# Adjacent heads on the two partition halves in a fused sigmoid attention and ReGLU kernel

## Chip, cores, metric

One core of one Trainium2 chip. The metric is the device time of one execution in microseconds (us).

## The reference, cut to what matters

```python
# q, k, v: [8 batches, 12 heads, 448, 64] fp32
scores = matmul(q, k.T) / sqrt(64) - log(448)
attn_out = matmul(1 / (1 + exp(-scores)), v)                  # no softmax, no row sums
x = attn_out.transpose(0, 2, 1, 3).reshape(3584, 768)         # heads side by side
out = (maximum(x @ w_gate, 0) * (x @ w_val)) @ w_out          # 768 -> 1536 -> 768
```

The head index is the upper part of the feature index of `x`. So heads 2j and 2j+1 together make up features 128j to 128j+127, one 128-row slice for the first matmul of the FFN.

## The kernel before

All matmuls are in fp16. For each batch the kernel loads k, q and v with a cast to fp16, transposes k and q, forms K·Qᵀ in 64x64 tiles (QK), applies the sigmoid on ScalarE (ACT), multiplies by v (PV), and mixes the FFN of an earlier batch into the gaps. Batch 0 has nothing to be mixed with: it runs as six "slots" of four QK units each, and FFN units (`"f"`: one 128-wide slice of the gate and value products) are placed among them by hand.

A tile holds two heads per partition half. Before, partitions 0 to 63 carry heads 0 to 5 and partitions 64 to 127 carry heads 6 to 11, so one load of a group of four heads is two transfers of 64 partitions:

```python
    def tiles_of(b):
        if b not in in_tiles:
            in_tiles[b] = tuple(
                inp.tile([P, NG, 2, NCH * D], FP16, tag=t, name=t) for t in ("k16", "q16", "v16")
            )
        return in_tiles[b]

    def rows_of(src, b, r, g0, g1, c0, c1):
        hs = src[b, 6 * r + 2 * g0 : 6 * r + 2 * g1]
        return hs.rearrange("h (t c) d -> t h (c d)", c=NCH)[:, :, c0 * D : c1 * D]

    def load(b, g0, g1, which="kqv", c0=0):
        for nm, t16, src in zip("kqv", tiles_of(b), (k, q, v)):
            if nm in which:
                for r in range(2):
                    nc.gpsimd.dma_start(
                        t16[64 * r : 64 * r + 64, g0:g1, :, c0 * D :].rearrange(
                            "t g h x -> t (g h) x"
                        ),
                        rows_of(src, b, r, g0, g1, c0, NCH),
                    )

    KCUT = 4                                   # the first k and q come as fp32 (QCUT is 3, NCH 7, D 64)
    first32 = []
    for src, c0, c1 in ((k, 0, KCUT), (q, 0, QCUT)):
        ysb = ysbp.tile([P, DM], FP32, tag="ysb", name="ysb")
        t32 = ysb[:, 0 : 2 * (c1 - c0) * D].rearrange("p (h x) -> p h x", h=2)
        for r, eng in ((0, nc.sync), (1, nc.scalar)):
            eng.dma_start(t32[64 * r : 64 * r + 64], rows_of(src, 0, r, 0, 1, c0, c1))
        first32.append(t32)
    # ... (constants)
    load(0, 0, 1, "k", KCUT)
    load(0, 1, 2, "kq")
    load(0, 2, 3, "kq")
    load(0, 0, 1, "q", QCUT)
    load(0, 0, 3, "v")
    # ... then the weights of the FFN by slices, with k and q of batch 1 between them
```

`load` issues everything on GpSimd's queue (POOL), in this order. A QK unit and a PV group use the four 64x64 quadrants of TensorE at once (in the profile of before, four PV matmuls of 448 columns start within 10 ns and the next four 189 ns later):

```python
    def qk(qkT, r, hh, c, c0, c1, out_ap):
        rows = slice(64 * hh, 64 * hh + 64)
        cols = slice(64 * r, 64 * r + 64)
        nc.tensor.matmul(
            out_ap,
            qkT[rows, c, cols],
            qkT[rows, NCH + c0 : NCH + c1, cols],
            start=True,
            stop=True,
            tile_position=(64 * hh, 64 * r),
            skip_group_check=True,
        )

    def pv(b, g, q0, qn, pieces):
        v16 = in_tiles[b][2]
        ps = [bank("pv_ps") for _ in range(2)]
        for c in range(NCH):
            for hh in range(2):
                for r in range(2):
                    rows = slice(64 * r, 64 * r + 64)
                    nc.tensor.matmul(
                        ps[r][64 * hh : 64 * hh + 64, 0:qn],
                        v16[rows, g, hh, c * D : (c + 1) * D],
                        pieces[c][rows, hh, :],
                        start=(c == 0),
                        stop=(c == NCH - 1),
                        tile_position=(64 * r, 64 * hh),
                        skip_group_check=True,
                    )
        for r in range(2):
            put_xT(b, NG * r + g, q0, qn, ps[r][:, 0:qn])
```

The places of PV and of FFN units among the six slots of batch 0 (transposes and warm-up matmuls cut):

```python
    push_first(0, range(0, 4), False)          # four FFN units for the first 192 rows
    after = {
        # ...
        (2, 2): slots[0].pv,
        (2, 3): slots[1].pv,
        (3, 1): slots[2].pv,
        (3, 3): lambda: ffn_mix("f"),
        (4, 0): lambda: ffn_mix("f"),
        (4, 1): slots[3].pv,
        (4, 3): lambda: ffn_mix("f"),
        (5, 0): lambda: ffn_mix("f"),
        (5, 1): slots[4].pv,
    }
    for i, slot in enumerate(slots):
        for u in range(4):
            slot.unit(u)
            if (i, u) in after:
                after[(i, u)]()
    slots[5].pv()
    # ...
    ffn_mix("ff", [(1, lambda: both(1, 0))])   # then batch 1
```

## Time and profile before

| kernel before | value |
|---|---|
| three timed executions | 433.53, 434.48, 434.69 us; median 434.48 |
| the profiled execution: time / span in the profile | 437.15 / 435.4 us |
| TensorE busy | 423.8 us, 97% of the span |
| first QK / fourth PV matmul ("full PV") / first FFN unit | 7.75 / 18.75 / 24.12 us |
| second half of v of batch 0 landed at | 18.71 us |

The span is what the profile covers, some 1.8 us less than the time of the same execution. TensorE works nearly all the time, so only its early holes can give anything; the "milestones" in the fourth row, taken from the start of the span, date them. PV of batch 0 starts with a few matmuls on the half of v that came first; the fourth needs the rest, so its start shows when v had landed.

### The profile page before, as it was taken

The numbers are of one execution on the slowest core, as the hardware profiler recorded it, in microseconds if no ns is written. First come the engines' busy times: TensorE is split into PE (matmuls) and PEld (weight loads), VectorE is DVE, ScalarE is ACT, GpSimd is POOL, SyncE is SP. The second block draws the span as 40 slices with busy tenths as digits, with TensorE's granted clock in tenths as the row PEclk, the third lists the DMA queues.
The fourth block names the chain that finished last, engine by engine and source line by source line (L and its number), as shares of the span: only waits on it lengthen the run. The fifth ranks groups of instructions, "written<-read, shape, count | busy, mean of one in ns | idle before, by whom it ended". The sixth has DMA issues, their size and how long they took to land.

```text
span 435.4 us, 8668 instructions
## 1 busy us (share of the span) xinstructions
PE 423.8 (97%) x3670; PEld 237.2 (54%) x3670; DVE 129.5 (30%) x246; ACT 212.0 (49%) x453; POOL 59.8 (14%) x97
## 2 busy tenths in 40 slices
PE   7789999999999999999999999999999999999996
PEld 3567776455555455455555555455555545555563
DVE  2243244222332323322332223323332222222111
ACT  4585778454554555654554635645654545122110
POOL 8555510621030000300030000100000000000000
PEclk9899999999999999999999999999999999999999
DMA  8999945999999043963259225631243101100144
GB/s 134 183 198 198 196 63 98 170 202 220 209 148 182 0 80 81 154 115 79 43 96 182 65 44 80 106 74 38 43 80 80 38 0 38 36 2 0 40 106 108
DMA packets 70214, 43.64 MB, mean 100 GB/s; under 512 B 35488, under 2 KB 66592, under 8 KB 70176
## 3 DMA queue, kind: packets, MB, share of 16 engines
q0 software_dynamic: 32128, 23.37, 36.6%
q1 hardware_dynamic: 37680, 19.44, 22.0%
q8 instruction: 28, 0.46, 0.4%
q10 hardware_dynamic: 368, 0.30, 0.3%
q14 instruction: 10, 0.08, 0.0%
HBM read 47.19 MB, written 11.01 MB: 134 GB/s over the span
## 4 chain that ended last, share of the span: by engine, by line
PE 93%; DMA 3%; ACT 1%; POOL 1%; DVE 1%; issue 1%; ACTq 0%; POOLq 0%
PE g_ps L292 26%; PE v_ps L292 25%; PE ya L330 17%; PE qk_ps L214 9%; PE yb L330 8%; PE pv_ps L231 7%; DMA v<-in_v_dram 2%; DMA k<-in_k_dram 1%; ACT PT L175 1%; DVE xT L166 1%; PE trt L189 1%; POOL k L97 0%; POOL v L97 0%; POOL q L97 0%; ACT ysb L344 0%
## 5 line engine op out<-in xcount | busy, mean ns | idle before, releaser
L175 ACT ACTIVATE PT<-qk_ps 128x448 f16<-128x448 f32 (+3 forms) x318 | 150.8, 594 | 38.3 <-PE qk_ps L214 38.3
L292 PE MATMUL g_ps<-xT,wg 128*128 128x448 f16 (+2 forms) x648 | 127.5, 332 | 0.6 <-DVE xT L166 0.4
L292 PE MATMUL v_ps<-xT,wv 128*128 128x448 f16 (+2 forms) x648 | 126.8, 332 | 0.0
L310 DVE TENSOR_TENSOR hT<-gate_sb,v_ps 128x448 f16<-128x448 f32 (+2 forms) x108 | 60.9, 568 | 195.7 <-PE v_ps L292 116.4
L301 ACT ACTIVATE gate_sb<-g_ps 128x448 f32<-128x448 f32 (+2 forms) x104 | 55.3, 543 | 74.7 <-PE g_ps L292 73.8
L330 PEld LDWEIGHTS <-hT 128*128 128x128 f16 x672 | 65.8, 98 | 47.0
L292 PEld LDWEIGHTS <-wv 128*128 128x128 f16 x648 | 62.5, 98 | 46.8
L292 PEld LDWEIGHTS <-wg 128*128 128x128 f16 x648 | 59.3, 98 | 49.2 <-issue 10.7
L330 PE MATMUL ya<-wo,hT 128*128 128x512 f16 x336 | 77.1, 379 | 0.0
L344 ACT ACTIVATE ysb<-yb 128x256 f32<-128x256 f32 x28 | 10.7, 383 | 102.1 <-PE yb L330 102.1
L214 PE MATMUL qk_ps<-qkT 64*64 64x448 f16 (+2 forms) x756 | 52.2, 339 | 2.3 <-ACT PT L175 1.3
L330 PE MATMUL yb<-wo,hT 128*128 128x256 f16 x336 | 41.3, 273 | 0.0
L231 PE MATMUL pv_ps<-PT,v 64*64 64x448 f16 (+2 forms) x756 | 38.3, 337 | 2.5 <-DMA v<-in_v_dram 2.1
L166 DVE TENSOR_SCALAR xT<-pv_ps 128x448 f16<-128x448 f32 (+2 forms) x54 | 28.4, 567 | 31.5 <-PE pv_ps L231 31.5
L214 PEld LDWEIGHTS <-qkT 64*64 64x64 f16 x756 | 21.3, 107 | 29.8 <-issue 21.2
L97 POOL DMA_DIRECT2D v<-in_v_dram x18 | 12.1, 680 | 177.4 <-PE qk_ps L214 169.7
L338 DVE TENSOR_SCALAR ysb<-ya 128x512 f32<-128x512 f32 x28 | 19.3, 691 | 55.2 <-PE ya L330 55.2
L231 PEld LDWEIGHTS <-v 64*64 64x64 f16 x756 | 22.6, 111 | 13.9 <-DMA v<-in_v_dram 2.5
L97 POOL DMA_DIRECT2D q<-in_q_dram x28 | 17.5, 644 | 7.1 <-DMA v<-in_v_dram 4.7
L97 POOL DMA_DIRECT2D k<-in_k_dram x28 | 17.5, 635 | 6.8 <-DMA wv<-in_moe_w_val_dram 3.8
L194 DVE COPY qkT<-trt 128x896 f16<-128x896 f16 (+2 forms) x14 | 7.5, 554 | 7.7 <-PE trt L189 7.5
L158 PE MATMUL warm_ps<-zeros 128*128 128x448 f16 x22 | 7.1, 451 | 1.2 <-DVE zeros L114 1.2
(24 smaller groups left out, 46.5 us busy)
## 6 DMA issues: line engine op xcount, KB each, us to landing
out_dram<-ysb SPq DMA_DIRECT2D x54, 192.0 KB, 2.7
v<-in_v_dram POOLq DMA_DIRECT2D x14, 336.0 KB, 7.0
k<-in_k_dram POOLq DMA_DIRECT2D x10, 336.0 KB, 9.0
q<-in_q_dram POOLq DMA_DIRECT2D x10, 336.0 KB, 13.4
wg<-in_moe_w_gate_dram POOLq DMA_DIRECT2D x6, 384.0 KB, 10.0
wv<-in_moe_w_val_dram POOLq DMA_DIRECT2D x6, 384.0 KB, 10.4
k<-in_k_dram POOLq DMA_DIRECT2D x16, 112.0 KB, 7.7
q<-in_q_dram POOLq DMA_DIRECT2D x16, 112.0 KB, 6.4
```

Of the source, the lines that this page charges most:

```text
L97: nc.gpsimd.dma_start(t16[64 * r : 64 * r + 64, g0:g1, :, c0 * D :].rearrange("t g h x -> t (g h) x"), rows_of(src, b, r, g0, g1, c0, NCH),)
L166: nc.vector.tensor_scalar(out=xT_of(b, pr)[:, q0 : q0 + qn], in0=src, scalar1=XSCALE, scalar2=None, op0=AOP.mult,)
L175: nc.scalar.activation(PT_ap, ps_ap, AF.Sigmoid, bias=sig_bias, scale=qk_scale)
L194: nc.vector.tensor_copy(qkT[:, ti * NCH + c0 : ti * NCH + c1, :].rearrange("p c x -> p (c x)"), trt[:, c0 * P : c1 * P],)
L214: nc.tensor.matmul(out_ap, qkT[rows, c, cols], qkT[rows, NCH + c0 : NCH + c1, cols], start=True, stop=True, tile_position=(64 * hh, 64 * r ...
L231: nc.tensor.matmul(ps[r][64 * hh : 64 * hh + 64, 0:qn], v16[rows, g, hh, c * D : (c + 1) * D], pieces[c][rows, hh, :], start=(c == 0), sto ...
L292: nc.tensor.matmul(ps[-1][:, 0:qn], wt[:, dc, f * P : (f + 1) * P], xT_tiles[(b, dc)][:, q0 : q0 + qn], start=(dc == 0), stop=(dc == NDC - 1),
L301: nc.scalar.activation(gate_sb[:, 0:qn], ps[0][:, 0:qn], AF.Relu)
L310: nc.vector.tensor_tensor(out=hT_tiles[(g, f)][:, o : o + qn], in0=gate_sb[:, 0:qn], in1=ps[1][:, 0:qn], op=AOP.mult,)
L330: nc.tensor.matmul(ps[:, 0 : m1 - m0], hT_tiles[(g, f)][:, t * P : (t + 1) * P], wo[:, f, m0:m1], start=(f == 0), stop=(f == NFC - 1),)
L338: nc.vector.tensor_scalar(out=ysb[:, m0:m1], in0=ps[:], scalar1=OUT_SCALE, scalar2=None, op0=AOP.mult)
L344: nc.scalar.activation(ysb[:, m0:m1], ps[:, 0 : m1 - m0], AF.Copy, scale=OUT_SCALE)
```

## The change

The intent is to let each k and q load cover all 128 partitions. Head 2x goes to partitions 0 to 63 and head 2x+1 to 64 to 127, so a group of heads is one transfer instead of two. The PV result of a pair of heads must land in the two halves of one PSUM tile. With v and the sigmoid on the same halves, that would use only the two diagonal quadrants. So odd pairs are exchanged: QK writes their results to the other partition half, and their v is loaded exchanged. In PV, both row halves now write the same PSUM bank, on different partitions. The patch also moves FFN work: six FFN units instead of four run among the first slots, two of them after the last QK unit, and one more before batch 1.

```diff
-                inp.tile([P, NG, 2, NCH * D], FP16, tag=t, name=t) for t in ("k16", "q16", "v16")
+                inp.tile([P, NPAIR, NCH * D], FP16, tag=t, name=t) for t in ("k16", "q16", "v16")
...
+    def rows_of(src, b):
+        return src[b].rearrange("(x r) (t c) d -> (r t) x (c d)", r=2, c=NCH)
...
-                for r in range(2):
-                    nc.gpsimd.dma_start(t16[64 * r : 64 * r + 64, g0:g1, ...], ...)
+                xs = slice(2 * g0, 2 * g1)
+                nc.gpsimd.dma_start(t16[:, xs, c0 * D :], rows_of(src, b)[:, xs, c0 * D :])
+
+    def load_v(b):
+        v16 = tiles_of(b)[2]
+        nc.gpsimd.dma_start(v16[:, 0::2, :], rows_of(v, b)[:, 0::2, :])
+        for r in range(2):
+            nc.gpsimd.dma_start(
+                v16[64 - 64 * r : P - 64 * r, 1::2, :], rows_of(v, b)[64 * r : 64 * r + 64, 1::2, :]
+            )
...  first fp32 loads: k whole on SP's queue, q whole on ACT's (were one half of each on both)
+    for src, c1, eng in ((k, KCUT, nc.sync), (q, QCUT, nc.scalar)):
...
+    load_gv(4, 6)
     load(1, 0, 1, "kq")
-    load_gv(4, 6)
...
+    def row_of(r, hh):
+        return 64 * (r if hh == 0 else 1 - r)
...  QK: output on partitions o = row_of(r, hh), tile position (64 * hh, o)
...  PV:
-                        ps[r][64 * hh : 64 * hh + 64, 0:qn],
-                        v16[rows, g, hh, c * D : (c + 1) * D],
+                        ps[hh][64 * r : 64 * r + 64, 0:qn],
+                        v16[rows, 2 * g + hh, c * D : (c + 1) * D],
-                        tile_position=(64 * r, 64 * hh),
+                        tile_position=(o, 64 * r),
...
-    push_first(0, range(0, 4), False)
+    push_first(0, range(0, 6), False)
...
-        (4, 3): lambda: ffn_mix("f"),
+        (4, 2): lambda: ffn_mix("f"),
         (5, 0): lambda: ffn_mix("f"),
         (5, 1): slots[4].pv,
+        (5, 3): lambda: ffn_mix("ff"),
...
-    ffn_mix("ff", [(1, lambda: both(1, 0))])
+    ffn_mix("fff", [(1, lambda: both(1, 0))])
...  batch 1: FFN units per stretch 3, 4, 3, 3, 2 instead of 4, 4, 3, 4, 3
...  loads of v and of the output weights for batch 2: v first
```

More of the change, by code (lines that the diff above doesn't have):

```diff
@@ L84, in tiles_of, with load @@
             in_tiles[b] = tuple(
-                inp.tile([P, NG, 2, NCH * D], FP16, tag=t, name=t) for t in ("k16", "q16", "v16")
+                inp.tile([P, NPAIR, NCH * D], FP16, tag=t, name=t) for t in ("k16", "q16", "v16")
             )
         return in_tiles[b]
-    def rows_of(src, b, r, g0, g1, c0, c1):
-        hs = src[b, 6 * r + 2 * g0 : 6 * r + 2 * g1]
-        return hs.rearrange("h (t c) d -> t h (c d)", c=NCH)[:, :, c0 * D : c1 * D]
-    def load(b, g0, g1, which="kqv", c0=0):
-        for nm, t16, src in zip("kqv", tiles_of(b), (k, q, v)):
-            if nm in which:
-                for r in range(2):
-                    nc.gpsimd.dma_start(
-                        t16[64 * r : 64 * r + 64, g0:g1, :, c0 * D :].rearrange(
-                            "t g h x -> t (g h) x"
-                        ),
-                        rows_of(src, b, r, g0, g1, c0, NCH),
-                    )
+    def rows_of(src, b):
+        return src[b].rearrange("(x r) (t c) d -> (r t) x (c d)", r=2, c=NCH)
+    def load(b, g0, g1, which, c0=0):
+        for nm, t16, src in zip("kq", tiles_of(b), (k, q)):
+            if nm in which:
+                xs = slice(2 * g0, 2 * g1)
[7 more added lines that the diff above has]
+            )
     KCUT = 4
     first32 = []
-    for src, c0, c1 in ((k, 0, KCUT), (q, 0, QCUT)):
+    for src, c1, eng in ((k, KCUT, nc.sync), (q, QCUT, nc.scalar)):
         ysb = ysbp.tile([P, DM], FP32, tag="ysb", name="ysb")
-        t32 = ysb[:, 0 : 2 * (c1 - c0) * D].rearrange("p (h x) -> p h x", h=2)
-        for r, eng in ((0, nc.sync), (1, nc.scalar)):
-            eng.dma_start(t32[64 * r : 64 * r + 64], rows_of(src, 0, r, 0, 1, c0, c1))
+        t32 = ysb[:, 0 : 2 * c1 * D].rearrange("p (x y) -> p x y", x=2)
+        eng.dma_start(t32, rows_of(src, 0)[:, 0:2, 0 : c1 * D])
         first32.append(t32)
@@ L122 @@
     load(0, 0, 1, "q", QCUT)
-    load(0, 0, 3, "v")
+    load_v(0)
     wg = wpool.tile([P, NDC, DF], FP16, name="wg")
@@ L142 @@
     load_gv(10, 12)
-    load(1, 0, 3, "v")
+    load_v(1)
     def load_o():
@@ L190, in pe_transposes @@
                     trt[64 * h : 64 * h + 64, c * P : (c + 1) * P],
-                    t16[:, g, h, c * D : (c + 1) * D],
+                    t16[:, 2 * g + h, c * D : (c + 1) * D],
                     ident[:],
@@ L204, in dma_transposes @@
                 rel[:, ti * NCH : (ti + 1) * NCH, :].rearrange("p c (h d) -> p h c d", h=2),
-                t16[:, g].rearrange("p h (c d) -> p h c d", c=NCH),
+                t16[:, 2 * g : 2 * g + 2, :].rearrange("p h (c d) -> p h c d", c=NCH),
             )
@@ L209, in dma_transposes, with qk @@
         )
-    def qk(qkT, r, hh, c, c0, c1, out_ap):
-        rows = slice(64 * hh, 64 * hh + 64)
-        cols = slice(64 * r, 64 * r + 64)
-        nc.tensor.matmul(
-            out_ap,
-            qkT[rows, c, cols],
-            qkT[rows, NCH + c0 : NCH + c1, cols],
-            start=True,
-            stop=True,
-            tile_position=(64 * hh, 64 * r),
-            skip_group_check=True,
-        )
+    def row_of(r, hh):
+        return 64 * (r if hh == 0 else 1 - r)
+    def qk(qkT, c, c0, c1, out_of):
+        for r in range(2):
+            for hh in range(2):
+                rows = slice(64 * hh, 64 * hh + 64)
+                cols = slice(64 * r, 64 * r + 64)
+                o = row_of(r, hh)
+                nc.tensor.matmul(
+                    out_of(hh)[o : o + 64, :],
+                    qkT[rows, c, cols],
+                    qkT[rows, NCH + c0 : NCH + c1, cols],
+                    start=True,
+                    stop=True,
+                    tile_position=(64 * hh, o),
+                    skip_group_check=True,
+                )
     def pv(b, g, q0, qn, pieces):
@@ L229, in pv @@
                 for r in range(2):
-                    rows = slice(64 * r, 64 * r + 64)
+                    o = row_of(r, hh)
+                    rows = slice(o, o + 64)
                     nc.tensor.matmul(
-                        ps[r][64 * hh : 64 * hh + 64, 0:qn],
-                        v16[rows, g, hh, c * D : (c + 1) * D],
+                        ps[hh][64 * r : 64 * r + 64, 0:qn],
+                        v16[rows, 2 * g + hh, c * D : (c + 1) * D],
                         pieces[c][rows, hh, :],
@@ L236, in pv @@
                         stop=(c == NCH - 1),
-                        tile_position=(64 * r, 64 * hh),
+                        tile_position=(o, 64 * r),
                         skip_group_check=True,
                     )
-        for r in range(2):
-            put_xT(b, NG * r + g, q0, qn, ps[r][:, 0:qn])
+        for hh in range(2):
+            put_xT(b, 2 * g + hh, q0, qn, ps[hh][:, 0:qn])
     class FirstSlot:
@@ L254, in unit @@
             for j, c in enumerate(cs):
-                for r in range(2):
-                    for hh in range(2):
-                        qk(
-                            qkT_tiles[(0, self.g)], r, hh, c, self.c0, self.c1,
-                            ps[64 * r : 64 * r + 64, hh, j * qn : (j + 1) * qn],
-                        )
+                qk(
+                    qkT_tiles[(0, self.g)], c, self.c0, self.c1,
+                    lambda hh: ps[:, hh, j * qn : (j + 1) * qn],
+                )
             PT = PTp.tile([P, 2, 512], FP16, tag="PT", name="PT")
@@ L274, in qk_unit @@
         ps = [bank("qk_ps") for _ in range(2)]
-        for r in range(2):
-            for hh in range(2):
-                qk(qkT_tiles[(b, g)], r, hh, c, 0, NCH, ps[hh][64 * r : 64 * r + 64, 0:S])
+        qk(qkT_tiles[(b, g)], c, 0, NCH, lambda hh: ps[hh][:, 0:S])
         PT = PTp.tile([P, 2, 512], FP16, tag="PT", name="PT")
@@ L377 @@
     k16, q16, _ = in_tiles[0]
-    nc.vector.tensor_copy(k16[:, 0, :, 0 : KCUT * D], first32[0])
-    nc.scalar.copy(q16[:, 0, :, 0 : QCUT * D], first32[1])
+    nc.vector.tensor_copy(k16[:, 0:2, 0 : KCUT * D], first32[0])
+    nc.scalar.copy(q16[:, 0:2, 0 : QCUT * D], first32[1])
     pe_transposes(0, 0, 0, 0, KCUT)
@@ L413 @@
     slots[5].pv()
-    push_first(1, range(0, 4))
-    for f0 in range(4, 12, 2):
+    push_first(1, range(0, 6))
+    for f0 in range(6, 12, 2):
         for half in range(2):
@@ L441, in late_loads @@
         hold(2, 1)
-        load(2, 0, 1, "v")
+        load_v(2)
         load_o()
-        load(2, 1, 3, "v")
-    ffn_mix("ff", [(1, lambda: both(1, 0))])
+    ffn_mix("fff", [(1, lambda: both(1, 0))])
     for b in range(1, B):
@@ L451 @@
         if b == 1:
-            mix = ["f" * n for n in (4, 4, 3, 4, 3)]
+            mix = ["f" * n for n in (3, 4, 3, 3, 2)]
             hooks = {
@@ L484 @@
                     hold(2, 2)
-                load(b + 1, 0, 3)
+                load(b + 1, 0, 3, "kq")
+                load_v(b + 1)
             ffn_mix(mix[m], hooks.get(m, ()))
```

## The prediction

> **What bounds the kernel now.** I read the page first: busy shares, the 40 slices, the chain that ended last. Its first and third parts say that TensorE is the bound for nearly the whole span, and its slices that DMA is busiest in the first eighth.
>
> ```profile
> span 435.4 us, 8668 instructions
> PE 423.8 (97%) x3670; PEld 237.2 (54%) x3670; DVE 129.5 (30%) x246; ACT 212.0 (49%) x453; POOL 59.8 (14%) x97
> PE   7789999999999999999999999999999999999996
> PE 93%; DMA 3%; ACT 1%; POOL 1%; DVE 1%; issue 1%; ACTq 0%; POOLq 0%
> ```
>
> The reader is to see that only the first three digits of the PE row, some 33 us, are under 9. The change removes no matmul, so a gain must come from there, or from a wait hidden inside a "busy" PE. To see which wait, I took the waits of PE and the timeline of PE for 17 to 22 us:
>
> ```profile
> PE pv_ps L231 <- DMA v<-in_v_dram: 2.1, 2, 1.1
> ...
> PE trt L189 <- ACT q L379: 1.1, 1, 1.1
> ```
>
> ```profile
> 17.34 0.27 PE L231 MATMUL pv_ps<-PT,v 64*64 64x192 f16 x1 [0.99 <-DMA v<-in_v_dram]
> 18.75 1.33 PE L231 MATMUL pv_ps<-PT,v 64*64 64x192 f16 x27 [1.14 <-DMA v<-in_v_dram]
> ```
>
> The two real waits of PE on a load are these: v of batch 0 (PE's earlier work ended at 16.34 us; apart from one matmul nothing runs until 18.75), and q of the first pair. Then four stretches around that hole, with the granted clock as last-but-two column:
>
> ```profile
> 11.50:14.90 3.40, 3.37 (x69) 1.70 (x70) 1.25 (x2) 2.78 (x4) 3.40 (x5) 1.00 1.17 173
> 14.90:18.30 3.40, 1.71 (x31) 0.72 (x27) 0.42 (x1) 2.29 (x3) 0.69 (x2) 1.00 1.37 187
> 18.30:21.70 3.40, 2.95 (x72) 2.95 (x76) 0.92 (x4) 0.49 (x1) 1.34 (x2) 0.50 1.45 197
> 21.70:25.10 3.40, 2.54 (x63) 1.96 (x55) 1.22 (x5) 3.21 (x4) 1.05 (x3) 1.00 1.39 200
> ```
>
> The stretch with the hole is followed by one at half clock (0.50). So the late v costs twice. Last, why v is late: the timeline of the first 40 us and the waits of the POOL queue.
>
> ```profile
> 1.49 2.51 POOL L97 DMA_DIRECT2D k<-in_k_dram  x4
> 6.27 1.87 POOL L97 DMA_DIRECT2D q<-in_q_dram  x3
> 9.04 1.34 POOL L97 DMA_DIRECT2D v<-in_v_dram  x2
> 20.95 0.84 POOL L131 DMA_DIRECT2D wg<-in_moe_w_gate_dram  x1 [1.37 <-DMA wg<-in_moe_w_gate_dram]
> 22.94 0.82 POOL L132 DMA_DIRECT2D wv<-in_moe_w_val_dram  x1 [1.15 <-DMA wv<-in_moe_w_val_dram]
> ```
>
> GpSimd issues without a pause from 1.49, twelve 64-partition loads of some 0.63 us each, and only at 9.04 gets to v. The last two lines also tell when the first weight pair had landed (20.7 and 22.7 us: [...]these two waited for the transfers eight places earlier).
>
> [...]152 GB/s and 172 GB/s written at 5 to 15 us. At 95 to 100 us, when nothing but 64-partition loads with six rows each are queued, it moves 204 GB/s, the same as full-width weights at 20 to 25 us (199). So the half-width itself isn't slow here[...]. [...]the k issue takes 635 ns for 64 x 2 rows, v 680 ns for 64 x 6, a weight slice 838 ns for 128 x 6, so most of an issue is a fixed cost and merging two nearly halves it.[...]
>
> **The change part by part.**
> First loads: k and q of the first pair (256 KB and 192 KB) now start together, k on the SP queue and q on ACT's, where q was second on both (issued 1.49, used at 6.38; k issued 0.74, used at 4.18). I put both landings at 4.5 to 4.7 us, an estimate from the 3.3 us that k took plus its doubled share of one queue. Then k's cast 0.67, its transposes 0.34, two warm matmuls 0.4, q's transposes 0.3 and the copy 0.36 put the first QK at about 6.85 where it was 7.75: 0.9 us earlier. From there to PV the chain is transposes, copies and sigmoids, 8.65 us, with no load wait in the trace; its loads keep pace if they come a microsecond sooner.
> Issue: twelve k/q issues of 0.63 become six of about 0.65 (a 256-row issue, between 0.635 and 0.838). v gets issued at 1.49 + 6 x 0.65 = 5.4 us instead of 9.04. Data then bounds it: 1.84 MB of k, q and v in fp16, at 200 GB/s from 3.2 us on is 9.2 us, with the share of the first fp32 loads (0.5 us)[...]: 14.5 to 16.5, middle 15.9. PV(0) could start at 16.4 - 0.9 = 15.5. So full PV starts at 15.9, not 18.75: **2.85 us gained**, of which 0.9 belongs to q.
> Clock: the half-clock stretch holds 18.75 to 21.7, with PV of two slots (7 quads each) and five QK quads. At 83 ns for a 192-column quad and 107 for a 256-column one that is about 1.7 us warm, 2.9 us measured: **1.2 us gained**[...].
> FFN order: the sum of FFN units is the same (24), but six instead of four run among the first slots. In those slots ACT is nearly full (12 sigmoids, 10.9 us of a 12.2 us stretch), and the two at the end lie beside the last sigmoids, where PE waits some 0.9 us now: **0.8 us gained**. But these units need weights of slices 2 and 3 (0-based f = 4, 5) early. With weights 1.7 to 4 us sooner than now, the first unit (24.1 now, about 20 then) and the fifth meet weights landing within a microsecond of them: **0.5 us lost**. In batch 1 fifteen units stay for 42 sigmoids (0.45 us each when back to back): ACT has 18.9 + 15 x 0.35 = 24.2 us of work in some 31 us, so PE stays the bound on average, but its last stretch has 4.5 + 0.7 us of ACT beside 4.6 of PE: **0.5 us lost**.
> QK and PV: the same 756 + 756 matmuls on the same four quadrants; only the order within a quad turns diagonal. In the trace four start within 10 ns and the next four 189 ns later, whatever the quadrant: **0**.
> Loads of batches 2 to 7: 6 transfers per batch become 5, off the path, in a stage where PE is 100% busy: **0**.
> Sum: 2.85 + 1.2 + 0.8 - 0.5 - 0.5 = 3.85 us. 434.48 - 3.85 = **430.6 us**, 0.9% faster.
>
> **The rivals.**
> A. Weights take v's place. All early data pass at about 200 GB/s, and that rate is reached already from 15 us on; faster issue only fills the 152 and 172 of 5 to 15 us. Bytes missing there are about 5 x (48 + 28) = 380 KB, 1.9 us of data. If arrival of weights, not v, then holds PE, the gain ends near 2 us: 432.5. For it: first use of weights at 24.1 against landing at 22.7, only 1.4 us of slack, all of which the earlier v uses up.
> B. The whole early stage was issue-bound, v comes at 14.5, the clock stays up, and the two extra FFN units vanish in ACT waits: 0.9 + 2.3 + 1.4 + 2 = 6.6 us, 428. Against it: the DMA share of 1.17 against 1.40 says that the engines had little left to give.
> C. PSUM. In PV both row halves now write one bank at the same time (hh = 0: tiles (0,0) and (64,64) into ps[0], other partitions). [...]the four no longer run together and PV, 28 us at 189 ns a quad, would double: some 460 us. Against it: one bank's two writers sit on different partitions, and in each column half the two row halves still use different banks. I give it 4%.
> D. The clock: [...]the 1.2 us stay lost.
>
> **Range and chances.** A and D give 432 to 433.5, B gives 428 and perhaps 427: 427 to 433.6 holds 8 in 10. Over 2% faster needs 425.8, beyond B: 4%. Slower by over 2% is C or a new stall in late weights: 5%.
>
> **What would show it.** After: first QK near 6.9 us; the PE waits on v gone or under 1 us; PEclk 1.00 from 5 us on; 5:15 at 180 GB/s or more; PV groups still 1.32 us for 28; QK and PV mean durations as before; in the second 90 us no change but a shift. Wrong if PE waits on wg, wv or wo appear with over 1 us, if the half-clock stretch stays, or if PV takes more than 189 ns a quad.

## The result, and the profile after

| | before | after |
|---|---|---|
| median of four executions (range), us | 434.59 (433.53 to 435.54) | 432.78 (432.71 to 433.13) |
| ratio after to before | | 0.9961, 95% interval 0.9937 to 0.9984 |
| time / span of the profiled execution, us | 437.15 / 435.4 | 432.71 / 430.9 |
| first QK / full PV / first FFN unit, us | 7.75 / 18.75 / 24.12 | 6.65 / 16.11 / 20.08 |

The change is worth 0.4%: 1.8 us by the medians, where I had said 3.85. But the two profiles differ by 4.5 us, and that contradiction is what the experiments had to settle.

The page of the kernel after, its lines on busy time, slices of PE and chain:

```profile
span 430.9 us, 8612 instructions
...
PE 422.5 (98%) x3670; PEld 235.5 (55%) x3670; DVE 130.6 (30%) x248; ACT 211.3 (49%) x451; POOL 50.5 (12%) x75
...
PE   8899999999999999999999999999999999999996
...
PE 94%; DMA 2%; POOL 1%; DVE 1%; ACT 1%; issue 0%; ACTq 0%; POOLq 0%
```

PE has as many matmuls as before (3670), and its first digits go from 7, 7, 8 to 8, 8, 9. GpSimd is busy for 50.5 us where it was 59.8. The waits of PE in the first 45 us of the kernel after (total, times, longest, in us), and its timeline around PV:

```profile
PE pv_ps L240 <- DMA v<-in_v_dram: 0.6, 1, 0.6
```

```profile
15.07 0.40 PE L240 MATMUL pv_ps<-PT,v 64*64 64x192 f16 x3
16.11 0.76 PE L240 MATMUL pv_ps<-PT,v 64*64 64x192 f16 x25 [0.64 <-DMA v<-in_v_dram]
...
20.08 0.67 PE L297 MATMUL g_ps<-xT,wg 128*128 128x192 f16 x6
```

The wait on v has shrunk from 2.1 to 0.6 us, the one on q is gone, and full PV starts at 16.11, where I had put it at 15.9. Three stretches of the kernel after (busy us and instructions of PE, PEld, DVE, ACT and POOL, then granted clock, DMA share and GB/s):

```profile
10.00:15.00 5.00, 4.66 (x93) 2.39 (x96) 1.51 (x4) 3.90 (x6) 3.28 (x4) 1.00 1.31 201
14.90:18.30 3.40, 2.76 (x113) 2.47 (x113) 1.67 (x5) 2.21 (x4) 2.03 (x3) 1.00 1.45 197
18.30:21.70 3.40, 2.51 (x47) 1.64 (x39) 1.33 (x4) 2.90 (x4) 1.08 (x3) 1.00 1.46 198
```

The clock is 1.00 throughout, and the DMA moves 201 GB/s from 10 to 15 us where it moved 172. GpSimd's queue shows what was done differently: the timeline of POOL in the kernel after, where v is issued at 5.92 instead of 9.04, and the issue of k in the groups of instructions (time in all and mean ns), which takes 777 ns for a whole width where it took 635 ns for a half.

```profile
1.49 1.59 POOL L97 DMA_DIRECT2D k<-in_k_dram  x2
...
5.92 0.77 POOL L101 DMA_DIRECT2D v<-in_v_dram  x1
```

```profile
L97 POOL DMA_DIRECT2D k<-in_k_dram x14 | 10.9, 777 | 6.2 <-PE v_ps L297 1.6
```

Last, the steady stage. The chain in order of time of the kernel before, then of the kernel after, at the same place in the work:

```profile
172.59 1.32 PE pv_ps L231 x28
173.92 0.81 PE qk_ps L214 x12
```

```profile
168.03 1.32 PE pv_ps L240 x28
169.36 0.81 PE qk_ps L222 x12
```

28 PV matmuls take 1.32 us in both. So rival C, a clash in PSUM, does not occur. From 105 to 375 us the two profiles take the same time for the same work; the difference lies ahead of that.

### The profile page after: what moved, and what is told of

The parts are those of the page before. It is cut to its first block, busy times and chain, and to the rows that moved or that the text cites. A ratio compares the mean times of both kernels' runs of the same rounds, so it can differ in the third digit from the quotient of the medians. Undisturbed runs are those within 1.5% of the kernel's fastest.

```text
span 430.9 us, 8612 instructions
## 1 busy us (share of the span) xinstructions
PE 422.5 (98%) x3670; PEld 235.5 (55%) x3670; DVE 130.6 (30%) x248; ACT 211.3 (49%) x451; POOL 50.5 (12%) x75
## 4 chain that ended last, share of the span: by engine, by line
PE 94%; DMA 2%; POOL 1%; DVE 1%; ACT 1%; issue 0%; ACTq 0%; POOLq 0%
PE g_ps L297 26%; PE v_ps L297 25%; PE ya L335 17%; PE qk_ps L222 9%; PE yb L335 9%; PE pv_ps L240 7%; DMA v<-in_v_dram 2%; DVE xT L168 1%; PE trt L191 1%; POOL k L97 1%; ACT PT L177 1%; POOL q L97 0%; POOL v L101 0%; POOL v L103 0%; ACT ysb L349 0%
## 5 line engine op out<-in xcount | busy, mean ns | idle before, releaser
L306 ACT ACTIVATE gate_sb<-g_ps 128x448 f32<-128x448 f32 (+2 forms) x102 | 54.4, 545 | 75.2 <-PE g_ps L297 73.2
L240 PE MATMUL pv_ps<-PT,v 64*64 64x448 f16 (+2 forms) x756 | 36.8, 329 | 0.6 <-DMA v<-in_v_dram 0.6
L240 PEld LDWEIGHTS <-v 64*64 64x64 f16 x756 | 21.4, 107 | 11.8 <-DMA v<-in_v_dram 0.8
L101 POOL DMA_DIRECT2D v<-in_v_dram x8 | 6.0, 747 | 172.4 <-PE qk_ps L222 172.1
L97 POOL DMA_DIRECT2D q<-in_q_dram x14 | 10.6, 759 | 9.9 <-DMA wo<-in_moe_w_out_dram 5.9
L97 POOL DMA_DIRECT2D k<-in_k_dram x14 | 10.9, 777 | 6.2 <-PE v_ps L297 1.6
L103 POOL DMA_DIRECT2D v<-in_v_dram x16 | 10.1, 635 | 2.2 <-DMA wg<-in_moe_w_gate_dram 1.3
```

Of the source, the lines that this page charges most:

```text
L97: nc.gpsimd.dma_start(t16[:, xs, c0 * D :], rows_of(src, b)[:, xs, c0 * D :])
L103: nc.gpsimd.dma_start(v16[64 - 64 * r : P - 64 * r, 1::2, :], rows_of(v, b)[64 * r : 64 * r + 64, 1::2, :])
L240: nc.tensor.matmul(ps[hh][64 * r : 64 * r + 64, 0:qn], v16[rows, 2 * g + hh, c * D : (c + 1) * D], pieces[c][rows, hh, :], start=(c == 0), ...
L306: nc.scalar.activation(gate_sb[:, 0:qn], ps[0][:, 0:qn], AF.Relu)
```

## The experiments

My theory after reading this: earlier v gives nearly all of the gain, and the first profile of before was an unlucky execution. The rivals: (R1) the clock gives a part of it in all executions; (R2) the first q gives a part; (R3) the FFN order gives it; (R4) v lands earlier for another reason than merged issues, such as the weights behind it or the moment of its own issue. Fourteen kernels ran, two of them repeats. All gave correct results.

| kernel | edit | us, median (range) | ratio to before, 95% |
|---|---|---|---|
| b_again | before, unchanged | 434.76 (433.56–437.23) | 1.0000 (0.9976–1.0024) |
| b_warm | idle matmuls in the hole | 435.07 (434.65–435.31) | 1.0002 (0.9986–1.0018) |
| a_oldffn | after, with the FFN order of before | 433.22 (432.92–433.29) | 0.9957 (0.9939–0.9974) |
| a_split | after, with halved k and q loads | 434.47 (434.11–435.26) | 0.9991 (0.9974–1.0008) |
| a_again | after, unchanged | 432.49 (432.28–432.74) | 0.9943 (0.9927–0.9958) |
| b_qfirst | before, with k and q first on own queues | 434.92 (434.09–436.53) | 1.0005 (0.9985–1.0025) |
| b_newffn | before, with the FFN order of after | 433.88 (433.59–434.20) | 0.9977 (0.9961–0.9993) |
| a_pvlater | after, PV of slots 0 and 1 one place later | 432.32 (432.14–432.94) | 0.9942 (0.9927–0.9957) |
| b_vgate | before, weights not issued until v has landed | 440.49 (440.25–441.20) | 1.0131 (1.0094–1.0168) |
| a_vgate | after, the same | 438.49 (437.73–439.52) | 1.0090 (1.0046–1.0135) |
| b_vlate | before, v issued 2 us later | 435.05 (434.39–435.57) | 1.0001 (0.9970–1.0032) |
| b_vlate_warm | both of b_vlate and b_warm | 434.90 (434.84–437.06) | 1.0014 (0.9981–1.0047) |
| a_wide1 | after, twelve whole-width loads of one row | 433.73 (432.71–435.29) | 0.9989 (0.9960–1.0019) |
| a_narrow4 | after, half-width loads of four rows, not more of them | 435.64 (434.86–436.21) | 1.0024 (0.9998–1.0051) |

The rows from b_again to a_split ran in one session, the next four in a second, then two, two and two. The milestones in the text are each from one profiled execution.

### b_again and a_again: is either profile typical?

No edit; the two kernels ran once more, with a profile.

> The kernel before once more, unchanged, for a second profile and more times. Theory 1 (the profile of before was an unlucky execution: its half-clock stretch and its latest v are not in most executions): ratio to before 1.000 within 0.3%, span of this profile 1.5 to 3.5 us under the 435.4 of the first one, no half-clock stretch between 15 and 25 us or a shorter hole before full PV (PV full start at 16.5 to 18 us). Theory 2 (every execution has hole and half clock, and the gain is lost later): span 434 to 436, half clock near 18 to 22 us again.

> The changed kernel once more, beside the other parts on one chip. Expected: ratio to before 0.995 to 0.997, times within 0.6 us of each other, no half clock between 15 and 25 us, full PV at 16.0 to 16.4 us. If its first look was the lucky one instead: 0.998 and more, or a half-clock stretch.

The timeline of PE of b_again, beside the same of before in the prediction (18.75):

```profile
15.82 0.24 PE L231 MATMUL pv_ps<-PT,v 64*64 64x192 f16 x1
...
17.32 0.77 PE L231 MATMUL pv_ps<-PT,v 64*64 64x192 f16 x27 [1.25 <-DMA v<-in_v_dram]
```

```profile
14.90:18.30 3.40, 2.15 (x74) 1.59 (x77) 0.60 (x2) 2.10 (x4) 1.35 (x3) 1.00 1.34 182
18.30:21.70 3.40, 2.51 (x84) 1.97 (x73) 1.70 (x6) 3.04 (x4) 0.96 (x2) 1.00 1.45 199
```

The same kernel, but full PV starts at 17.32, and no half-clock stretch follows (the 1.00 in both stretches of its windows). Its span is 432.5 us, against 435.4 in the first profile. a_again, by contrast, repeats the profile of after: full PV at 16.03 (16.11 before), span 430.8 (430.9). So the first profile of before was the unlucky one; against a usual execution v gains about 1.2 us, not 2.64.

How often is it unlucky? Of the 39 executions of the unchanged kernel before in these sessions, 5 have a mean granted clock (the share of its full clock that TensorE was given; 0.50 is half clock) of 0.996 or less. Of the 21 executions of after, a_oldffn, a_again and a_pvlater, none has (all 0.998 or more). The times of each of these kernels lie within 0.4 to 0.8 us, those of before within 1.8 to 3.7 us in each session. The clock is not all of this scatter: in 7 of the 39 executions the time exceeds the span by 2.8 to 3.3 us, in the others and in all 21 by 1.7 to 2.0, so some of it lies outside what the profile covers.

### b_warm, b_vlate, b_vlate_warm: what is the clock worth? (R1)

```diff
# b_warm, on the kernel before
-        (2, 2): slots[0].pv,
+        (2, 2): lambda: (keep_warm(10), slots[0].pv()),
# b_vlate, on the kernel before, ahead of the load of v of batch 0
+    delay = const.tile([P, P], FP16, name="delay")
+    for _ in range(8):
+        nc.gpsimd.memset(delay[:], 0.0)
# b_vlate_warm: both
```

> The kernel before with ten idle 448-column matmuls (some 1.9 us warm) between the last QK of slot 2's third unit and the first PV, so that the array works while it waits for v and the clock stays up. Theory 1 (the clock drops only in some executions): 0.0 to 0.6 us faster than before in the median, and times closer together than before's. Theory 2 (it drops in every execution and costs 1.2 us): 1.0 to 1.4 us faster. In both the profile shows granted clock 1.00 from 5 us on and PV still held by v.

> The kernel before with eight small GpSimd memsets (about 1.6 us) ahead of the issue of v: it makes on purpose the late v that the first profile had by chance. If that profile is explained by a late v plus half clock: v landed and full PV at 18.4 to 19 us, a half-clock window in most executions (mean clock 0.996 or less), and 1.5 to 3 us slower than before, 436.3 to 437.5. If the tail of slow engines, not the issue, sets v's landing: full PV still at 17.2 to 17.6 and no slower.

> The same late v, with ten idle matmuls in the hole that it makes. If the half clock costs 1.2 us on top of the hole: clock 0.998 or more in all executions and 0.8 to 1.4 us faster than the late v without them. If the clock costs nothing: within 0.3 us of it.

b_warm fills the hole: from 14.90 to 18.30 us PE is busy for all of the 3.40 us, and the clock stays at 1.00, but the time is unchanged (1.0002). The idle matmuls ran on past the landing of v, though (landed 17.50, PV from 17.96), so this test alone could hide a gain of up to 0.5 us; the clock of 1.00 after the hole in b_again is the better evidence that a usual execution has no such loss. The delayed v of b_vlate brought the half clock in two of its four executions, but not the 1.5 to 3 us that I had expected of it (1.0001). Its profile is one of those; PE's wait on v, and the stretch after the hole:

```profile
PE pv_ps L234 <- DMA v<-in_v_dram: 2.0, 1, 2.0
```

```profile
18.30:21.70 3.40, 3.40 (x105) 3.40 (x96) 1.24 (x4) 1.94 (x3) 1.35 (x2) 0.59 1.44 193
```

The two executions with a clock of 0.994 took 435.49 and 435.57 us, the two with 1.0 took 434.60 and 434.39: a half-clock stretch costs about 1.0 us, close to the 1.2 of my prediction. It may not all be the clock's, for the hole may have been longer in the same two, and the ratios cannot check it: theirs are uncertain by 0.3%. With a frequency of 5 in 39, this is 0.1 us on average and nothing in the median. b_vlate_warm, with the hole filled (but with v in its profile at 17.27, no later than in b_again), took 434.84 to 434.93 us in three of four executions, between the two groups of b_vlate; the fourth (437.06, clock 0.996) shows that filling this one hole does not prevent every loss of clock. R1 is true of some executions only.

Why of some only? In the trace of before the granted clock is at half from 18.30 to 21.72 us, in that of b_vlate from 18.93 to 22.34: for 3.41 us in both, but not at the same time after the start. So each trace is divided here in steps of 3.41 us from a recorded change of its own clock, and not, as above, at the same times for all. Divided so, b_vlate, b_again and a_wide1 (below; v at 18.73) have these stretches in the hole:

```profile
15.51:18.93 3.42, 1.42 (x61) 1.18 (x61) 0.58 (x2) 1.37 (x3) 2.46 (x5) 1.00 1.34 185
```

```profile
14.61:18.03 3.42, 2.17 (x63) 1.34 (x66) 0.42 (x1) 2.29 (x3) 1.51 (x3) 1.00 1.32 180
```

```profile
13.82:17.23 3.41, 2.32 (x38) 0.90 (x36) 0.80 (x2) 2.74 (x5) 1.05 (x2) 1.00 1.18 161
17.23:20.65 3.42, 2.26 (x88) 1.95 (x90) 1.10 (x4) 0.61 (x2) 2.23 (x3) 1.00 1.44 196
```

Half clock followed the stretches with PE busy for 1.72 us (before, 14.89 to 18.30), 1.42 (b_vlate) and 1.84 (a_vgate, 7.28 to 10.69) of 3.41; after those with 2.17 (b_again), 2.32 and 2.26 us (a_wide1) the clock was 1.00. In a_wide1 a boundary falls into the hole and splits it: v as late as in before (18.73 against 18.71 us), and no half clock. That the place of the boundary made the difference is my reading of these few stretches and not shown; no run moved it on purpose.

### b_qfirst: the first q (R2)

```diff
# on the kernel before
-    for src, c0, c1 in ((k, 0, KCUT), (q, 0, QCUT)):
+    for src, c0, c1, eng in ((k, 0, KCUT, nc.sync), (q, 0, QCUT, nc.scalar)):
...
-        for r, eng in ((0, nc.sync), (1, nc.scalar)):
+        for r in range(2):
```

> The kernel before with its first k (both halves) on the SP queue and its first q (both halves) on ACT's; nothing else. If the earlier q is hidden behind the wait for v: q used 0.5 to 1 us earlier, full PV unchanged at 17.2 to 17.6 us, ratio 0.999 to 1.001. If it is worth the 0.9 us of my sum: full PV near 16.5 us and ratio 0.998.

Nothing: 1.0005. The wait on q was gone from its profile, but full PV still started where it did in b_again, because v still lands last:

```profile
17.11 0.77 PE L231 MATMUL pv_ps<-PT,v 64*64 64x192 f16 x27 [0.72 <-DMA v<-in_v_dram]
```

But first QK was at 7.72 us in this profile, no earlier than in b_again (7.39): k was now what PE waited for (1.0 us). So the edit only shows that other queues for the first k and q gain nothing in the old layout; it did not bring what R2 is about, an earlier first QK. For that, compare after and a_again: first QK at 6.65 and 7.29 us, full PV at 16.11 and 16.03, time 432.71 and 432.59 us. PE that starts 0.64 us earlier arrives earlier at the same wait for v. Over all profiles first QK moved between 6.1 and 7.8 us. So R2 finds no support.

### a_oldffn and b_newffn: loads alone, FFN order alone (R3)

a_oldffn is the kernel after with the FFN order and the order of the gate and value weights taken from before; b_newffn is the reverse. In short:

```diff
# b_newffn, on the kernel before (a_oldffn is the reverse of it on after)
-    push_first(0, range(0, 4), False)
+    push_first(0, range(0, 6), False)
-        (4, 3): lambda: ffn_mix("f"),
+        (4, 2): lambda: ffn_mix("f"),
+        (5, 3): lambda: ffn_mix("ff"),
-    ffn_mix("ff", [(1, lambda: both(1, 0))])
+    ffn_mix("fff", [(1, lambda: both(1, 0))])
     # and the order of the weight loads, the split of the later units and the mix of batch 1
```

> The changed kernel with the FFN order and the weight order of before (four units among the first slots, two before batch 1, 4-4-3-4-3 in it): loads alone. If the FFN order is worth what I said (0.8 gained, 1.0 lost) it is within 0.4 us of the changed kernel: ratio to before 0.995 to 0.997. If the FFN order carries the gain: ratio 0.998 to 1.000. If the FFN order costs time: ratio under 0.994.

> The kernel before with the FFN order and the weight order of the changed kernel; loads as before. If the new order pays by itself: ratio 0.997 to 0.999. If it needs the earlier weights: PE waits of over 0.5 us on wg or wv among the first slots, ratio 1.000 to 1.004. In the sum I had +0.8 and -1.0 us, thus 1.000.

The loads alone give 0.9957 (1.9 us of 434.8), the FFN order alone 0.9977 (1.0 us). Both together give 0.9961 and 0.9943 in two measurements, 1.7 and 2.5 us; the sum of the parts, 2.9 us, is somewhat above, within what the intervals of the three ratios leave open. So R3 is partly true, and my own net of -0.2 us for this part had the wrong sign. Where it comes from is seen in the timelines of PE, first b_again (the order of before), then b_newffn:

```profile
29.91 0.63 PE L231 MATMUL pv_ps<-PT,v 64*64 64x256 f16 x16
30.79 0.79 PE L231 MATMUL pv_ps<-PT,v 64*64 64x256 f16 x12 [0.24 <-ACT PT L175]
```

```profile
29.49 0.67 PE L292 MATMUL g_ps<-xT,wg 128*128 128x192 f16 x6
...
31.57 0.96 PE L231 MATMUL pv_ps<-PT,v 64*64 64x256 f16 x28
```

In the old order the last PV of batch 0 stands and waits for the last two sigmoids: it needs from 29.91 to 31.58 us where 0.96 would do. In the new order two FFN units run from 29.49 to 31.5 us, and PV then goes through in one piece. The first QK of batch 1 starts 2.26 us later (37.86 against 35.60), with 3.3 us more of FFN work done (two units of some 1.0 us and one of 1.3), so 1.0 us is gained. By the last output matmul 0.7 us of it is left (started at 427.68 against 428.40), so batch 1 gives some 0.3 back. No wait of PE on a weight appears in b_newffn or in after, where I had feared 0.5 us.

### a_split: after, with the k and q loads halved again

```diff
-                nc.gpsimd.dma_start(t16[:, xs, c0 * D :], rows_of(src, b)[:, xs, c0 * D :])
+                for r in range(2):
+                    hs = slice(64 * r, 64 * r + 64)
+                    nc.gpsimd.dma_start(
+                        t16[hs, xs, c0 * D :], rows_of(src, b)[hs, xs, c0 * D :]
+                    )
```

> The changed kernel with each k and q load of GpSimd as two 64-partition transfers again (layout, first loads, v and FFN order stay). If merged loads bring v sooner: v issued near 9 us again, full PV 1 to 2.5 us later than the 16.1 of the changed kernel, ratio to before 0.998 to 1.000. If the width is worth nothing and the earlier q and the FFN order carry the gain: ratio within 0.1% of the changed kernel's 0.996.

Everything but the merging is kept, and the gain is nearly gone: 0.9991. The waits of PE in its first 45 us, and its stretch from 10 to 15 us:

```profile
PE pv_ps L244 <- DMA v<-in_v_dram: 0.9, 2, 0.6
...
PE v_ps L301 <- DMA wv<-in_moe_w_val_dram: 0.6, 1, 0.6
PE trt L195 <- DMA q<-in_q_dram: 0.4, 1, 0.4
```

```profile
10.00:15.00 5.00, 4.26 (x80) 2.08 (x82) 1.88 (x3) 3.50 (x5) 4.95 (x7) 1.00 1.17 170
```

The rate is that of before (170 against 172), and GpSimd issues without a pause again (busy 4.95 of 5 us, against 3.28 in after). v lands at 16.80, and weights and q hold PE as well. So the new FFN order, the new layout and the new first loads together gave 0.4 us by the ratio. Whether the FFN order is worth less here than on the layout of before (1.0 us) is not shown: the intervals (0.9974 to 1.0008, 0.9961 to 0.9993) overlap.

### b_vgate and a_vgate: are the weights behind v what delays it? (R4)

```diff
# b_vgate, after the load of v of batch 0 and ahead of the weights (a_vgate: three copies)
+    vgate = const.tile([P, 2], FP16, name="vgate")
+    for r in range(2):
+        p = slice(64 * r, 64 * r + 1)
+        nc.gpsimd.tensor_copy(vgate[p, :], in_tiles[0][2][p, 0, 0, 0:2])
```

> The kernel before with GpSimd held, by two tiny copies that read v, until v of batch 0 has landed; only then are the weights issued. A diagnosis of what delays v, not a faster kernel. If the weights queued behind v take DMA time that v needs: v lands 1 to 2.5 us sooner than the usual 17.1 to 17.5, at 15 to 16 us, and full PV starts there. If v is late for its own issue and bytes alone: still 17 us or later. In both the weights come some 2 to 4 us later, PE waits for wg or wv before the first FFN unit, and the kernel is 1 to 3 us slower than before.

> The same hold in the changed kernel (three tiny copies, one for each v transfer). If weights behind v delay it: v lands at 14 to 15 us instead of 16.0 and PV starts when compute is ready, 15.1 to 15.7 us. If the early stream is simply full (1.84 MB at 200 GB/s): v lands within 0.4 us of 16.0. Weights later by 3 to 5 us, PE waits for them, 2 to 4 us slower than the changed kernel.

With no weight in the queue behind it, v of b_vgate landed at 17.22 us, where b_again had 17.28; a_vgate had 15.65, where after had 16.07 and a_again 15.98. So traffic behind v takes at most some 0.4 us from it in these profiles. The price for late weights was high: the wait of PE in b_vgate is

```profile
PE g_ps L296 <- DMA wg<-in_moe_w_gate_dram: 3.0, 1, 3.0
```

and the mean clock was 0.990 to 0.992 in all eight executions. Both became slower than before, by 1.3% and 0.9%, more than I had expected. b_vlate, above, tests the other half of R4: with v issued 2 us later (10.96 instead of 8.94), its last half landed at 17.93 instead of 17.28 us, and its first half at 15.37 instead of 15.36. (In b_vlate_warm, with v issued at 10.85, the last half landed at 17.27.) So a later issue hardly moves v. An issue earlier than in before was not tried alone: wherever six loads are ahead, v is also issued at 5.5 to 5.9 us instead of 8.6 and later, so the smaller number and the earlier issue that comes with it are tested together.

### a_wide1 and a_narrow4: width or number of transfers?

```diff
# a_wide1, in load(), on after: batch 0 only, one head row per transfer
+                step = 1 if b == 0 else 2 * (g1 - g0)
+                for x0 in range(2 * g0, 2 * g1, step):
+                    xs = slice(x0, x0 + step)
# a_narrow4, on after: pairs 2 to 5 of batch 0 as four half-width transfers of four rows
-    load(0, 1, 2, "kq")
-    load(0, 2, 3, "kq")
+    for t16, src in zip(tiles_of(0), (k, q)):
+        for r in range(2):
+            hs = slice(64 * r, 64 * r + 64)
+            nc.gpsimd.dma_start(t16[hs, 2:6, :], rows_of(src, 0)[hs, 2:6, :])
```

> The changed kernel with each k and q load of batch 0 from GpSimd cut by head instead of by half: 128 partitions with one row each, so twelve issues of the same bytes as in the kernel before, but all of full width. If full width is what brings the early data sooner: about 200 GB/s at 10 to 15 us, v landed and full PV at 15.8 to 16.3 us, within 0.3 us of the changed kernel. If the number of issues is: 150 to 175 GB/s at 5 to 15 us, full PV at 16.8 us or later as with narrow pairs, and a ratio to before of 0.998 or more.

> The changed kernel with k and q of batch 0's second and third pair as four 64-partition transfers of four rows: as few issues as the changed kernel has, but half width. q of the second pair comes later in this order, so PE is held near 9 us by 1 to 2 us and the time itself tells little; what counts is the data. If width decides: under 180 GB/s at 10 to 15 us and v landed at 16.6 us or later. If the number of issues decides: about 200 GB/s and v landed at 15.9 to 16.2 us.

The stretch from 10 to 15 us of a_wide1 (full width, twelve transfers of at most 112 KB), then of a_narrow4 (four of its six transfers half width, 224 KB each), with the latter's longest wait of PE:

```profile
10.00:15.00 5.00, 4.25 (x84) 2.07 (x78) 2.18 (x4) 3.54 (x7) 4.87 (x7) 1.00 1.14 151
```

```profile
10.00:15.00 5.00, 3.19 (x46) 1.68 (x46) 0.62 (x1) 1.58 (x3) 3.48 (x5) 0.68 1.32 201
```

```profile
PE trt L193 <- DMA q<-in_q_dram: 1.6, 1, 1.6
```

With half width in few transfers the queue moves 201 GB/s, as in after, and v landed at 15.37. With full width in many it moves 151 GB/s, and v landed at 18.73. These five microseconds are mostly v's: the four half-width transfers of a_narrow4 landed from 7.52 to 10.96. From 5 to 10 us, while k and q move, it is 177 GB/s against 161, and the ranges overlap: 165 to 184 in all profiles with six early loads, 150 to 174 in those with twelve. a_narrow4 is slow in spite of its v, because q of the second group comes with that of the third: PE waits 1.6 us for it, and the clock halves after that hole (0.68 on average in the stretch above). Here a caution is due: the profile of a_wide1 was taken from the slowest of its four executions (435.29 us), and its fastest, 432.71, equals the changed kernel. So the many small transfers make a late v likely rather than certain.

All profiles together say the same. In the ten profiles with twelve early k and q loads (before and all its variants, a_split, a_wide1) the last of v landed at 16.80 to 18.73 us. In the six profiles with six such loads (after, a_again, a_oldffn, a_pvlater, a_vgate, a_narrow4) it landed at 15.37 to 16.17. The ranges do not overlap, whatever the width. The last of k and q, however, landed at 11.68 to 12.31 us with six loads and at 11.70 to 13.17 with twelve (12.00 in a_wide1, 11.98 in after): fewer loads did not bring k and q sooner in general, only v behind them. The rate from 10 to 15 us alone is not enough to tell the landing: b_qfirst moved 189 GB/s there and still had v at 17.07.

### a_pvlater: can a better place for PV gain more?

```diff
-        (2, 2): slots[0].pv,
-        (2, 3): slots[1].pv,
+        (2, 3): slots[0].pv,
+        (3, 0): slots[1].pv,
```

> The changed kernel with each of the first two PV groups one unit later, so that QK of the last unit of slot 2 and its sigmoid run while v is still on its way. If v's landing still holds PV and ACT is the next bound among the first slots: full PV at the same 16.1 us, the ACT hole before it (0.8 us) gone, 0.4 to 1.0 us faster than the changed kernel. If the wait for v is no longer what holds the first stage: within 0.2 us of it.

0.9942, against 0.9943 of after in the same session: nothing. Taking PV out of the way of the last wait on v (0.6 us in after) does not turn into time. No kernel beats the changed one beyond the noise.

## Why the prediction was wrong, by its own steps

The predicted time was 430.6 us, and 432.78 was measured. That is inside the range, but the change itself was 1.8 us (2.4 in the repeat), not 3.85.

**The landing of v: "full PV starts at 15.9, not 18.75: 2.85 us gained".** This step failed, and it is the largest. Its first half came out: 16.11 and 16.03 were measured. That was partly luck, for my own terms (3.2 + 9.2 + 0.5 us) give 12.9, and what I put on top to reach 15.9 was an estimate that no trace shows; and two more things were off: the six issues took 4.43 us instead of 3.9, so v was issued at 5.92 instead of 5.4, and from 5 to 10 us the queue moved 184 GB/s instead of 200. Its second half was not a property of the kernel but of one execution. Usual profiles of the old loads show 17.11 to 17.32 (b_again, b_newffn, b_qfirst, b_vgate), so the term measures 1.0 to 1.3 us in place of 2.85. A warning was in my hands: the profiled execution took 437.15 us, the median 434.48, and my mechanism, 2.85 + 1.2 us, was read from an execution that was 2.7 us slow. (A smaller slip of reading: the last digit of its PE row, 6, is under 9 too; both kernels have it, and nothing rests on it.)

**"of which 0.9 belongs to q".** Wrong as well. First QK did come near the predicted 6.85 (6.65 in the first profile, but 7.29 in a_again), yet the earlier of the two gained nothing over the other (432.71 and 432.59 us). The wait for v, the last of the loads, swallowed what came early ahead of it.

**Clock, "1.2 us gained".** The size was about right where it occurs (about 1.0 us in b_vlate), but it occurs in 5 of 39 executions, so the median gains nothing. The change does seem to remove it: 0 of 21 executions of after, its repeat and the two variants that leave its loads as they are.

**FFN order, "0.8 gained, 0.5 lost, 0.5 lost".** The gain is right (1.0 us up to batch 1). The loss on weights did not come (no such wait), and the loss in batch 1 is about 0.3 us. Net, the term is +0.6 to +1.0 us in place of -0.2.

With the measured terms the sum is 1.0 to 1.3 for v, 0.1 for the clock on average, 0.6 to 1.0 for the FFN order: 1.7 to 2.4 us, against 1.8 and 2.4 measured. The intervals of the ratios are some 0.7 us wide to each side, so the agreement is no proof of each term.

**QK and PV, later loads: "0".** Right: 1.32 us for 28 PV matmuls in both, and the same chain in the steady stage. **Rival C** did not happen. **Rival A** named nearly the right time (432.5), but for the wrong reason: no weight ever held PE in after. **Rival B** fell with the landing of v. **Rival D** saw that the clock term could be lost, but as a half clock that stays in after; it was lost because before seldom has one.

**Open.** Shown is that the merging of k and q loads gives most of the gain, and that the landing of v goes with the number and size of the transfers ahead of it. Not shown is why. The pace of issue would fit (an estimate: 112 KB in 0.635 us is 181 GB/s, near the 163 to 189 of the kernel before), but then the 2 us delay of b_vlate should have moved v by about 2 us, and it moved by 0.65 us at most. Nor do k and q themselves land sooner with fewer transfers. An earlier issue of v with twelve loads ahead was not tried. Nor is it settled why one kernel's v landed at 18.71 us in the first profile of before and at 17.28 in b_again.

## What to carry to other kernels

Before sizing a wait from a profile, compare the time of the profiled execution with the median of the timed ones (here 437.15 against 434.48 us): a hole that only a slow execution has is not there to be gained. In a short start-up stage, merge early loads into fewer and larger ones for the sake of their number (here v landed at 15.37 to 16.17 us behind six of them, at 16.80 to 18.73 behind twelve; why it counts is open), and look for the load that lands last: here an earlier first QK gained nothing ahead of it. Where an engine waits for a last result (here PV for the last sigmoids), two units of independent work at that place were worth a microsecond.
